# A decode kernel's key and value tiles, each loaded in two halves on two queues

## The chip, the cores and the metric

The kernel runs on one core of one Trainium2 chip. The metric is the device time of one execution in microseconds. The time before is the median of three runs, 663.4 us (663.39 to 663.56).

## The reference

The layer adds three things: its input, an attention over a long cache for one new token, and a small gated MLP. There are 4 sequences (B), 32 heads (H) of 128 elements (Dh), 4096 cached positions (S) and a model width D of 640. All tensors are bf16.

```
xn  = layernorm(x)                                  # x: 4 x 1 x 640
q   = (xn @ wq) as 4 x 32 x 1 x 128
s   = einsum("bhqd,bhkd->bhqk", q, k_cache) / sqrt(128)
o   = einsum("bhqk,bhkd->bhqd", softmax(s), v_cache)
A   = o as 4 x 1 x 4096 @ wo
z   = gelu(xn @ w_in);  z1, z2 = halves of z        # 640 -> 1728 -> 2 x 864
B   = (z1 * (w_sp * layernorm(z2) + b_sp)) @ w_out
out = x + A + B
```

k_cache and v_cache have 4 x 32 x 4096 x 128 elements each, 134 MB each. Every element is read once and used for one multiply and add, so almost all the bytes that the kernel moves are these two.

## The kernel before

**Tiles.** The 32 heads are cut in eight groups of four. One group of one sequence is a tile, so there are NT = 32 key tiles and 32 value tiles, numbered i = 4 * group + sequence. A tile is contiguous in memory, 4 MB, and is laid over 128 lanes, each of which holds NC = 128 positions ("chunks") of one head, that is 16384 elements or 32 KB. HC = NC / 2 = 64 chunks are half of a lane.

**Slots.** Keys and values share a pool of KV_SLOTS = 5 slots of 32 KB a lane (`kv`, function `slot`). At the start three of them hold the weights: two hold wq, one holds w_in and w_out.

**Loads.** The function `load` takes a slot and starts the transfer of one tile on SyncE's queue (line 123). It is one transfer of 128 lanes by 32 KB, except for the last value tile, which goes in four cuts at the chunks V_CUTS = (0, 64, 96, 112, 128), so that work on it can begin before all of it is there. The list `loads` gives the order: k0, k1, v0, k2, v1, k3, and so on, with a second key tile in a row at two places (EXTRA_K), so that the values end last. `pump` walks along this list and starts a load when the slot's former tile has been marked in `used`. Pieces of the output weight `wo` (640 KB each, line 159; the last one in four parts, line 157) go on SyncE's queue too, after the loads of every fourth iteration, and two more at the end. ScalarE's queue carries only x, two scalars and half of the output.

**The loop.** Under `manual_schedule` the instructions of TensorE (PE), VectorE (DVE), ScalarE (ACT) and SyncE (SP) stand in each engine's stream in the order in which the Python code calls them. One iteration i does, for key tile i and, one step behind, value tile j = i - 1 (from the two extra key tiles on, two and three steps behind):

- `product(i, 0)` and `product(i, 1)` (L457, DVE): each half of the keys times the query, in place.
- `fold_half(i, 0/1)` (L466, DVE): adds the upper 64 of 128 elements to the lower 64, in place.
- `sums(i, 0/1)` (L475, PE): adds what is left down to 8 columns, with the identity as weights; `row_sums` (L486, DVE) adds these.
- For tile i - 1: `lane_max` (L495, DVE), `lay_max` (L501, ACT), `spread_max` (L508, PE), `head_max` (L515, DVE), then `exps` (L524, ACT; and L533 on GpSimd (POOL), which lays the probabilities out in `pm`).
- `blocks(j)` (L548, PE): the probabilities times value tile j, into `pv_acc`. After each second tile ACT copies it out (L558) and `gather` (L569, PE) picks the parts.
- At the end of the iteration `used` gets value tile j and key tile i, and `pump` runs: it starts the loads of v(i+1), into the slot that value tile j leaves, and of k(i+3), into the slot of key tile i.

After the loop come the last softmax, `blocks(30)`, the first cut of `blocks(31)`, `pairs` for the other cuts (L581), and the projections with the last two `wo` pieces (L647).

**Waits of a transfer.** A transfer that is issued waits, on the issuing engine's stream, for the instructions that last read its slot. It also takes one of eight completion semaphores in turn, and waits until that semaphore's former transfer has landed. What stands behind it in that engine's stream waits with it.

**The start.** x is loaded on ACT's queue; wq, w_in and w_out on SP's. ACT computes `rstd` of the layernorm (L251) first; PE then waits for wq (`q_ps`, L285), `stage_q(0)` spreads the first queries, and `gmlp()` does the mixer, all ahead of `product(0, 0)` in DVE's stream.

Of the kernel before, what the change touches and what calls it, by code (L numbers as in the profile page):

```python
# [21 lines left out]
def kernel(  # L22
# [14 lines left out]
    nc = tc.nc  # L37
# [13 lines left out]
    NT = HG * Bsz  # L51
    LN = P // HT
    NC = HT * S // P
    HC = NC // 2
# [25 lines left out]
    def slot(name):  # L80
        return kv.tile([P, SLOT], BF16, tag="kv", name=name)
# [27 lines left out]
    def kv_view(cache, i):  # L109
        hg, b = divmod(i, Bsz)  # L110
        return cache[b, HT * hg : HT * (hg + 1)].rearrange("h s d -> (h s) d").rearrange(
            "(p c) d -> p (c d)", c=NC
        )

    k_tiles, v_tiles = {}, {}
    V_CUTS = (0, 64, 96, 112, NC)

    def load(which, i):
        cache, tiles = (A_k_cache, k_tiles) if which == "k" else (A_v_cache, v_tiles)
        t = slot("k_nat" if which == "k" else "v_nat")  # L120
        cuts = V_CUTS if (which, i) == ("v", NT - 1) else (0, NC)
        for c0, c1 in zip(cuts, cuts[1:]):
            nc.sync.dma_start(  # L123
                out=t[:, c0 * Dh : c1 * Dh], in_=kv_view(cache, i)[:, c0 * Dh : c1 * Dh]
            )
        tiles[i] = t[:].rearrange("p (c d) -> p c d", d=Dh)
# [13 lines left out]
    def pump():  # L140
        while n_loaded[0] < len(loads):
            at = n_loaded[0] + 3 - KV_SLOTS
            if at >= 0 and occupants[at] not in used:
                return
            load(*loads[n_loaded[0]])
            n_loaded[0] += 1
# [134 lines left out]
    for c in range(DC):  # L281
        t, i = wq_parts[c]
# [488 lines left out]
```

## Time and profile before

| what | value |
|---|---|
| median of 3 runs | 663.4 us |
| the profiled execution's own time | 663.4 us |
| its span on the core | 661.6 us |
| busy: PE / DVE / POOL / ACT | 53% / 74% / 23% / 7% |
| bytes moved, mean rate | 282.57 MB, 427 GB/s |
| mean granted TensorE clock | 0.726 |

The span runs from the first to the last instruction of the profiled execution, and the execution's own time is 1.8 us longer. Each engine's busy time is without its waits. In the profile, L123 is line 123 of the kernel before; SPq and ACTq are instructions of those engines' sequencers, which issue transfers; q1 is SP's queue and q10 ACT's. A view that lists waits gives the waiting group, who released it, the time in total, the number of times and the longest. A line of the timeline gives the start, the duration, the engine and line, the tiles written and read, and in brackets the engine's idle time before it and who ended it. A line of the transfers gives the number of issues, KB of each and the median time from issue to landing.

### The profile page before, as it was taken

How to read it: one execution, taken by the hardware profiler on the slowest of the kernel's cores; microseconds unless marked ns; L12 is line 12 of the kernel's file. 1: busy time of each engine (PE TensorE's matmuls, PEld its weight loads, DVE VectorE, ACT ScalarE, POOL GpSimd, SP SyncE). 2: the span in 40 equal slices, each digit the busy share in tenths (PEclk: the TensorE clock that was granted, in tenths of full speed). 3: DMA queues.
4: the chain of work that ended last, by engine and by line, in shares of the span. 5: the costliest groups of instructions: out<-in, count | busy, mean ns of one | idle time of the engine just before them, and what ended most of it. 6: DMA issues, size and time to landing. Idle time of an engine off the chain costs nothing.

```text
span 661.6 us, 5115 instructions
## 1 busy us (share of the span) xinstructions
PE 348.7 (53%) x2109; PEld 144.6 (22%) x2109; DVE 491.5 (74%) x334; ACT 49.3 (7%) x138; POOL 151.3 (23%) x57
## 2 busy tenths in 40 slices
PE   2526653646445455663745654465643756435567
PEld 1402211212121121221212222121211312112124
DVE  2299797867789677788776698776787899777950
ACT  0201100001000010001000000000100000000010
POOL 3002222112222112222112222112222133122230
PEclk9999676776767777766678657777576577688585
DMA  9999999999999999999999999999999999999997
GB/s 368 432 438 429 430 440 427 440 423 434 442 416 447 424 433 442 423 440 424 433 440 423 440 428 431 442 421 442 422 435 442 422 441 428 427 442 428 429 428 289
DMA packets 11971, 282.57 MB, mean 427 GB/s; under 512 B 1344, under 2 KB 1964, under 8 KB 3244
## 3 DMA queue, kind: packets, MB, share of 16 engines
q1 hardware_dynamic: 11928, 282.25, 99.2%
q8 instruction: 16, 0.26, 0.1%
q14 instruction: 7, 0.06, 0.0%
q10 hardware_dynamic: 20, 0.01, 0.0%
HBM read 282.24 MB, written 0.01 MB: 427 GB/s over the span
## 4 chain that ended last, share of the span: by engine, by line
issue 49%; DMA 25%; POOL 15%; DVE 7%; PE 3%; SPq 1%; ACT 0%; POOLq 0%; DVEq 0%; ACTq 0%
DMA k_nat<-in_A_k_cache_dram 20%; POOL pm L533 15%; DMA wo<-in_A_wo_dram 4%; DVE k_nat L457 4%; DVE k_nat L466 2%; PE s_ps L475 2%; PE pv_acc L548 1%; SPq L123 0%; DVE s_sb L486 0%; PE out_ps L647 0%; PE pv L569 0%; POOL own_sum L593 0%; DVE m L495 0%; SPq L92 0%; SPq L104 0%
## 5 line engine op out<-in xcount | busy, mean ns | idle before, releaser
L457 DVE TENSOR_TENSOR k_nat<-k_nat,qbc 128x8192 bf16<-128x8192 bf16 x64 | 282.8, 4419 | 97.8 <-DMA k_nat<-in_A_k_cache_dram 97.8
L533 POOL TENSOR_TENSOR pm<-p,hmask_bf 128x512 bf16<-128x512 bf16 x32 | 142.5, 4452 | 490.9 <-ACT p L524 490.9
L475 PE MATMUL s_ps<-k_nat,ident 128*128 128x512 bf16 x512 | 189.2, 536 | 68.2 <-DVE k_nat L466 68.2
L466 DVE TENSOR_TENSOR k_nat<-k_nat 128x4096 bf16<-128x4096 bf16 x64 | 151.8, 2372 | 0.0
L548 PE MATMUL pv_acc<-v_nat,pm 128*32 128x512 bf16 x1008 | 88.6, 514 | 39.1 <-POOL pm L533 35.5
L508 PE MATMUL max_ps<-lay,head_scale 128*128 128x32 f32 x64 | 18.7, 383 | 171.4 <-ACT lay L501 171.4
L475 PEld LDWEIGHTS <-ident 128*128 128x128 bf16 x512 | 67.9, 135 | 171.1 <-issue 153.8
L508 PEld LDWEIGHTS max_ps<-lay,head_scale 128*128 128x128 f32 x64 | 14.6, 284 | 186.0 <-ACT lay L501 186.0
L548 PEld LDWEIGHTS <-pm 128*32 128x32 bf16 x1008 | 30.2, 120 | 96.2 <-POOL pm L533 52.0
L486 DVE TENSOR_REDUCE s_sb<-s_ps 128x64 f32<-128x512 f32 x64 | 43.3, 677 | 4.2 <-PE s_ps L475 4.2
L501 ACT ACTIVATE lay<-lane_diag,m 128x32 f32<-128x32 f32 x32 | 10.3, 321 | 395.9 <-DVE m L495 395.9
L602 DVE RECIPROCAL rden<-den 128x16 f32<-128x16 f32 x8 | 2.1, 257 | 32.2 <-PE den L600 32.2
L569 PE MATMUL pv<-sel,pv_sb 128*128 128x8 f32 x128 | 19.4, 279 | 9.3 <-ACT pv_sb L558 9.3
L569 PEld LDWEIGHTS pv<-sel,pv_sb 128*128 128x128 f32 x128 | 17.9, 217 | 17.2 <-ACT pv_sb L558 17.2
L524 ACT ACTIVATE p<-s_sb,nb 128x128 bf16<-128x128 f32 x32 | 12.9, 402 | 63.5 <-DVE nb L515 63.5
L558 ACT COPY pv_sb<-pv_acc 128x512 f32<-128x512 f32 x16 | 9.4, 585 | 91.8 <-PE pv_acc L548 91.8
L495 DVE TENSOR_REDUCE m<-s_sb 128x1 f32<-128x128 f32 x32 | 9.1, 286 | 1.1
L285 PE MATMUL q_ps<-wq,xnT 128*32 128x512 bf16 x40 | 4.5, 631 | 8.3 <-DMA wq<-in_A_wq_dram 8.3
L647 PE MATMUL out_ps<-wo,o_r 128*4 128x320 bf16 x56 | 8.0, 433 | 0.3 <-DMA wo<-in_A_wo_dram 0.3
L292 DVE CAST q_sb<-q_ps 128x512 bf16<-128x512 f32 x1 | 0.7, 691 | 9.3 <-PE q_ps L285 9.3
L515 DVE TENSOR_REDUCE nb<-max_ps 128x1 f32<-128x32 f32 x32 | 5.9, 183 | 0.9 <-PE max_ps L508 0.9
L607 DVE TENSOR_TENSOR o_n<-pv,rden 128x16 bf16<-128x16 f32 x8 | 1.3, 168 | 6.7 <-PE pv L581 6.7
(94 smaller groups left out, 91.4 us busy)
## 6 DMA issues: line engine op xcount, KB each, us to landing
k_nat<-in_A_k_cache_dram SPq DMA_DIRECT2D x32, 4096.0 KB, 37.9
v_nat<-in_A_v_cache_dram SPq DMA_DIRECT2D x31, 4096.0 KB, 33.6
wo<-in_A_wo_dram SPq DMA_DIRECT2D x7, 640.0 KB, 38.1
wq<-in_A_wq_dram SPq DMA_DIRECT2D x1, 4096.0 KB, 12.8
w_sb<-in_B_w_in_dram SPq DMA_DIRECT2D x1, 2160.0 KB, 19.5
v_nat<-in_A_v_cache_dram SPq DMA_DIRECT2D x1, 2048.0 KB, 24.5
wq<-in_A_wq_dram SPq DMA_DIRECT2D x1, 1024.0 KB, 14.8
v_nat<-in_A_v_cache_dram SPq DMA_DIRECT2D x1, 1024.0 KB
```

Source lines behind the costliest of these rows:

```text
L457: nc.vector.tensor_tensor(out=t, in0=t, in1=qbcs[i // Bsz][:, i % Bsz, None, :].to_broadcast([P, HC, Dh]), op=ALU.mult,)
L466: nc.vector.tensor_tensor(out=t[:, :, 0:HD2], in0=t[:, :, 0:HD2], in1=t[:, :, HD2:Dh], op=ALU.add)
L475: nc.tensor.matmul(out=s[:], lhsT=ident[:], rhs=t[:, :, g * RW : (g + 1) * RW], start=(g == 0), stop=(g == n - 1),)
L486: nc.vector.tensor_reduce(out=scores[i][:, half * HC : (half + 1) * HC], in_=sums_ps.pop((i, half))[:], axis=AX.X, op=ALU.add,)
L495: nc.vector.tensor_reduce(out=m1[:], in_=scores[i][:], axis=AX.X, op=ALU.max)
L501: nc.scalar.activation(out=d[:], in_=lane_diag[:], func=ACT.Copy, scale=maxes[i][:, 0:1])
L508: nc.tensor.matmul(out=ps[:], lhsT=head_scale[:], rhs=maxes[i][:], start=True, stop=True)
L524: nc.scalar.activation(out=p[:], in_=scores.pop(i)[:], func=ACT.Exp, bias=nb[:], scale=scale_qk, accum_out=acc[hg % NACC][:, b : b + 1],)
L533: nc.gpsimd.tensor_tensor(out=p_m[b][:, :, e : e + GC * HT].rearrange("p g (c h) -> p g c h", h=HT), in0=p[:].rearrange("p (g c) -> p g c" ...
L548: nc.tensor.matmul(out=pv_acc[g * LN : (g + 1) * LN, :], lhsT=pm[:, c // GC, :], rhs=v_nat[:, c : c + GC, :].rearrange("p c d -> p (c d)") ...
L558: nc.scalar.copy(out=pv_sb[:], in_=pv_acc[:])
L569: nc.tensor.matmul(out=pvs[hg][:, :, b - 1 : b + 1], lhsT=pv_sb[:, k * Dh : (k + 1) * Dh], rhs=sel[:, k, :, :], start=(k == 0), stop=stop ...
```

## The change

Every tile but the last value tile is loaded in two transfers of 128 lanes by 16 KB: the first 64 chunks of each lane on SyncE's queue, the other 64 on ScalarE's. The last value tile keeps its four cuts, all on SyncE's queue, and so do the weights.

```
     def load(which, i):
         cache, tiles = (A_k_cache, k_tiles) if which == "k" else (A_v_cache, v_tiles)
         t = slot("k_nat" if which == "k" else "v_nat")
-        cuts = V_CUTS if (which, i) == ("v", NT - 1) else (0, NC)
+        last = (which, i) == ("v", NT - 1)
+        cuts = V_CUTS if last else (0, HC, NC)
         for c0, c1 in zip(cuts, cuts[1:]):
-            nc.sync.dma_start(
+            eng = nc.scalar if c0 == HC and not last else nc.sync
+            eng.dma_start(
                 out=t[:, c0 * Dh : c1 * Dh], in_=kv_view(cache, i)[:, c0 * Dh : c1 * Dh]
             )
         tiles[i] = t[:].rearrange("p (c d) -> p c d", d=Dh)
```

As built, the streams of PE, DVE and POOL hold the same instructions in the same order. SP's stream has 63 transfers of half the size where it had 63 whole ones. ACT's stream has 63 transfers more: tile k0's half right behind `rstd`, k1's behind the copy of the first spread queries (L453), and in the loop those of v(i+1) and k(i+3) at the end of iteration i, behind `exps(i - 1)` and the copy L558 and ahead of `lay_max(i)`. There are still eight completion semaphores, so a transfer now waits for the one eight before it in a sequence in which most tiles count twice.

More of the change, by code (lines that the diff above doesn't have):

```diff
@@ L120, in load @@
         t = slot("k_nat" if which == "k" else "v_nat")
-        cuts = V_CUTS if (which, i) == ("v", NT - 1) else (0, NC)
+        last = (which, i) == ("v", NT - 1)
+        cuts = V_CUTS if last else (0, HC, NC)
         for c0, c1 in zip(cuts, cuts[1:]):
-            nc.sync.dma_start(
+            eng = nc.scalar if c0 == HC and not last else nc.sync
+            eng.dma_start(
                 out=t[:, c0 * Dh : c1 * Dh], in_=kv_view(cache, i)[:, c0 * Dh : c1 * Dh]
```

## Prediction

> **What bounds the kernel now.** I read the page's slices and queues first, then the transfers' time to landing, then the waits, then the last 60 us line by line. The page:
>
> ```profile
> span 661.6 us, 5115 instructions
> ...
> DMA  9999999999999999999999999999999999999997
> ...
> DMA packets 11971, 282.57 MB, mean 427 GB/s; under 512 B 1344, under 2 KB 1964, under 8 KB 3244
> ...
> q1 hardware_dynamic: 11928, 282.25, 99.2%
> ...
> q10 hardware_dynamic: 20, 0.01, 0.0%
> ```
>
> Every slice has the DMA engines 90% busy or more, but for the last. Queue 1 (SP's) holds them for 99.2% of 16 engines' span; queue 10 (ACT's) moves x and four small things. The window from 100 to 600 us moves 433 GB/s at a DMA share of 1.00. So the sum of packet times is the time, plus some 2 us before the first packet and 4 us after the last load. Is there ever too little queued?
>
> ```profile
> k_nat<-in_A_k_cache_dram SPq DMA_DIRECT2D x32, 4096.0 KB, 37.9
> v_nat<-in_A_v_cache_dram SPq DMA_DIRECT2D x31, 4096.0 KB, 33.6
> wo<-in_A_wo_dram SPq DMA_DIRECT2D x7, 640.0 KB, 38.1
> ```
>
> A tile of 4.19 MB needs 9.7 us at 433 GB/s, yet lands 34 to 38 us after its issue: three to four tiles are always queued. The waits say the same from the other side:
>
> ```profile
> ACT lay L501 <- DVE m L495: 395.9, 32, 23.3
> ...
> DVE k_nat L457 <- DMA k_nat<-in_A_k_cache_dram: 97.8, 25, 5.6
> ```
>
> DVE, the busiest engine (74%), waits some 4 us for nearly every k tile, and ACT idles 12.4 us (395.9/32) per tile ahead of `lay`. The page's chain gives "issue" 49% and POOL's `pm` 15%; with the queue never empty I read that as a pipeline paced by landings. The end, from the timeline:
>
> ```profile
> 606.54 4.43 DVE L457 TENSOR_TENSOR k_nat<-k_nat,qbc 128x8192 bf16<-128x8192 bf16 x1 [2.45 <-DMA k_nat<-in_A_k_cache_dram]
> ...
> 635.60 1.91 PE L548 MATMUL pv_acc<-v_nat,pm 128*32 128x512 bf16 x32 [0.53 <-DMA v_nat<-in_A_v_cache_dram]
> ...
> 639.17 1.89 PE L475 MATMUL s_ps<-k_nat,ident 128*128 128x512 bf16 x8
> ...
> 645.28 3.60 PE L548 MATMUL pv_acc<-v_nat,pm 128*32 128x512 bf16 x32 [2.30 <-DMA v_nat<-in_A_v_cache_dram]
> ...
> 650.15 1.90 PE L548 MATMUL pv_acc<-v_nat,pm 128*32 128x512 bf16 x16 [0.72 <-DMA v_nat<-in_A_v_cache_dram]
> ```
>
> k tile 30 lands at 606.5, and from there DVE works through tiles 30 and 31 with no idle time until 636.9, PE through blocks, sums and the last softmax. PE then waits for v tiles 29, 30 and the first cut of 31 only 0.53 + 2.30 + 0.72 = 3.5 us in all. So compute follows the DMA closely at the end: **slack 3.5 us**.
>
> The profiled execution took 663.4 us, 1.8 more than its span; that is also the median of the three runs, so sums are made against 663.4. About 0.2% (1.3 us) is what a measurement of this kernel can tell from no change.
>
> **The change part by part.**
>
> *Packets.* 63 tiles go from one transfer to two. The trace's packet records show one packet per lane and transfer: 32 KB takes 1213 ns, and the only 16 KB ones on this queue (the first cut of v tile 31) take 611 ns. Per engine and tile that is 8 x 1213 against 16 x 611: +72 ns; a second completion packet adds 9 ns. Times 63: **+5.1 us** at most. The records overlap slightly: in the steady part they sum to 1.0035 of the time, and where only 16 KB packets run (645 to 647 us) to 1.006. So a packet occupies about 1209 and 607.4 ns: 16 x 607.4 - 8 x 1209 = +46 ns, and with the rest of the completion packet's 9 ns some 50 ns; over 63 tiles about +3. I take **+2.8 us**, since it comes from the rate really reached. Ends: -2.5 (below, if turns hide the fixed part) to +5.1.
>
> *The turns between the queues.* The nearest row: from 6.57 to 10.21 us ACT's queue had two tiny transfers waiting beside wq's 32 KB packets. Its four packets (2 and 4 B) went at 6.567, 7.782, 8.998 and 10.213 us, one between every two of SP's, 1215 ns apart. So turns alternate one packet each, and a turn and back costs 2 ns beyond SP's 1213, packet included. Other rows are dearer: a 16 KB instruction fetch on q8 takes 879 to 1013 ns and the packet behind it 1681 to 1766, some 0.8 us lost. I take 0, from the ACT row, which is the queue used here; the dear end is a rival.
>
> *Equal turns, unequal queues.* This is the part I expect to hurt. A tile is usable when both halves are in. SP still carries all that ACT doesn't: 8.6 MB of weights at the start and seven `wo` pieces. A `wo` piece is 8 packets of 5 KB per engine; in their turns ACT sends 8 packets of 16 KB, a whole half tile (2.1 MB, 4.85 us). Each `wo` therefore sets SP's halves one half tile behind ACT's; six come before k tile 30, so the lag grows until ACT's queue runs dry. There, ACT holds just the two newest halves (4.2 MB). At 37.9 us x 433 GB/s, 16.4 MB are outstanding at an issue; landed halves that wait for their partner take the lag L from it. SP holds 16.4 - L - 4.2, ACT 4.2, and their difference is L: L = 4.0 MB, **9.3 us**. While it lasts no byte is lost: one non-empty queue fills the engines, and 12 MB stay queued. But k tile 30 is complete only L after its place in the total order. Ends 0 and 9.3; behind the sixth `wo` (issued 480.3) no new one comes, so ACT may run dry and SP regain some: I take **7.3 us**.
>
> *At the end.* SP alone holds v tile 31 and the last `wo`s, so total bytes still end in the same place (+2.8). Compute starts its last run from k tile 30 later by 7.3 + 2.6 (the share of packet cost by then) = 9.9 us; the 3.5 us of slack absorb their part. **+6.4 us**, which hides the +2.8 of the DMA's own end.
>
> *ACT's stream.* 63 triggers at 0.33 us (SP's own rows) make 21 us on an engine that is 7% busy. As built, a v and a k half stand behind `exps` and ahead of the next `lay`. The v half waits for `blocks` on PE, the k half for the sums of the old k tile: `lay` needs the next DVE reduction, which lies behind those sums and 4.4 us of product. A half waits also for the transfer eight before it on its semaphore, four tiles back, three where a `wo` lies between; on ACT that tile is, in the loop, nearly always one that DVE's product needs first. 0 us; without that cover 0.66 us per tile.
>
> *The start.* ACT issues tile 0's half after `rstd` (3.92 us) and takes turns with wq: w_in, at 21.1 us now, comes up to 4.9 us later, and with it the mixer; the first product then starts near 36 instead of 34.5. 30 us of queued loads cover it: 0. SP's shorter waits gain nothing.
>
> Sum: 663.4 + 6.4 = **669.8 us**.
>
> **Rivals.**
> 1. *Faster: the alternating turns hide each packet's fixed part.* The 16 and 32 KB records differ by 602 ns for 16 KB, so about 9 ns of each is fixed; in the ACT row above a 9 ns packet cost 2. If a 16 KB packet among turns costs 602, a tile's 16 cost 9632 against 8 x 1209 = 9672: -40 ns, x 63 = -2.5 us. With no lag (SP catching up whenever ACT's queue is empty) that is **660.9**. It decides only if the lag at k tile 30 is under the 3.5 us of slack. Against: six `wo`s. 11%.
> 2. *Packets alone, the halves in step*: **666.2**, or 668.5 with records that don't overlap. For it: ACT's queue is empty often, if ACT issues late. 15%.
> 3. *No change*: one set of engines, full either way: **663.4**. For it: DMA share 1.00 now. Against: 611 is more than half of 1213. 5%. The Trainium skill (DMA: Bandwidth & Descriptors, Rules for kernel authors) says that spreading DMAs over SP and ACT doesn't help bandwidth, since all run on the same 16 engines, and saves only issue time; by it the sum is 663.4, SP's 0.33 us issues being hidden. The trace agrees that the engines are full, and by its packet lengths differs on zero.
> 4. *A turn between two large packets costs something*: 10 ns a turn is 63 x 16 x 10 ns = 10 us, **680** with the lag; the q8 rows' 0.4 us a turn would be over 1000. For it, those rows; against, the ACT row. 10%.
>
> Forecast 59%, 667 to 675.
>
> **Numbers.** Likeliest 669.8. The range takes in rivals 2 and 3 in the main, the forecast and the mild part of rival 4: 663 to 680. Faster by over 0.2% is rival 1 with a little of 3: 0.12; within: 0.05; slower: the rest, 0.83.
>
> **What would show it.** Queue 10 with about 130 MB; 16 KB packets near twice the length by record while both queues wait, and a steady rate 0.3 to 0.5% under 433. ACT's halves landing some 10 to 20 us after issue, SP's over 30, and the product of an iteration waiting for SP's half. k tile 30's first product near 616; PE's waits for v at the end gone; a last slice emptier of DMA. Wrong if the halves land together, if the steady rate moves by over 1%, or if the end keeps its 3.5 us of waits.

## The result, and the profile after

The changed kernel takes 666.8 us (median of 4 runs, 666.39 to 667.34) against 663.5 before: a ratio of 1.0049, with a 95% interval of 1.0037 to 1.0062. It is slower by 3.3 us, where the prediction gave 6.4. The profiled execution took 666.4 us with a span of 664.6. The page's lines that answer to those of before:

```profile
span 664.6 us, 5294 instructions
...
DMA  9999999999999999999999999999999999999996
...
DMA packets 21044, 282.59 MB, mean 425 GB/s; under 512 B 2352, under 2 KB 2972, under 8 KB 4252
...
q1 hardware_dynamic: 11928, 150.13, 53.0%
...
q10 hardware_dynamic: 9092, 132.13, 46.5%
```

The same bytes go in 21,044 packets instead of 11,971, shared between two queues that together hold the engines for 99.5% of the span. The DMA is as full as before, and the span ends 3.0 us later. The transfers of the same page, with the median time from issue to landing last:

```profile
k_nat<-in_A_k_cache_dram ACTq DMA_DIRECT2D x32, 2048.0 KB, 22.2
k_nat<-in_A_k_cache_dram SPq DMA_DIRECT2D x32, 2048.0 KB, 37.3
v_nat<-in_A_v_cache_dram SPq DMA_DIRECT2D x32, 2048.0 KB, 32.5
v_nat<-in_A_v_cache_dram ACTq DMA_DIRECT2D x31, 2048.0 KB, 18.5
wo<-in_A_wo_dram SPq DMA_DIRECT2D x7, 640.0 KB, 42.1
```

ACT's halves land some 14 to 15 us sooner after their issue than SP's. A tile needs both, so the product waits for SP's half: DVE waits 25 times for a key tile as before, 100.7 us in all (97.8 before), but the longest wait is now 10.2 us (5.6 before). The end, from the timeline:

```profile
615.84 4.43 DVE L459 TENSOR_TENSOR k_nat<-k_nat,qbc 128x8192 bf16<-128x8192 bf16 x1 [2.47 <-DMA k_nat<-in_A_k_cache_dram]
...
642.30 3.84 PE L550 MATMUL pv_acc<-v_nat,pm 128*32 128x512 bf16 x64
...
647.80 1.89 PE L477 MATMUL s_ps<-k_nat,ident 128*128 128x512 bf16 x8
...
651.54 1.91 PE L550 MATMUL pv_acc<-v_nat,pm 128*32 128x512 bf16 x32
...
654.10 1.05 PE L550 MATMUL pv_acc<-v_nat,pm 128*32 128x512 bf16 x16
...
659.58 1.23 PE L649 MATMUL out_ps<-wo,o_r 128*4 128x320 bf16 x8 [0.55 <-DMA wo<-in_A_wo_dram]
```

Line against line: k tile 30's first product is 9.3 us later (615.84 against 606.54), the last sums 8.6 (647.80 against 639.17), the first cut of v tile 31 only 3.95 (654.10 against 650.15), and the output projection 2.9 (659.58 against 656.64). Compute starts its last run 9.3 us late and ends it 2.9 late. It has made good 6.4 us, more than the 3.5 us of waits for v, and those waits are gone from all three lines. Two of the blocks are also shorter: those of tile 30 take 1.91 us where they took 3.60, the first cut 1.05 where it took 1.90.

What ends last is told by the chain of waits in order of time (start, duration, what the time went to). Before, from its end:

```profile
628.55 28.05 DMA wo<-in_A_wo_dram
656.60 0.04 issue
656.64 2.34 PE out_ps L647 x16
```

And after:

```profile
609.98 33.19 DMA v_nat<-in_A_v_cache_dram
643.17 0.02 issue
643.19 16.34 DMA wo<-in_A_wo_dram
659.54 0.04 issue
659.58 2.34 PE out_ps L649 x16
```

In both kernels the end waits for the last pieces of `wo` to land: the DMA's own end sets the time, not the computation behind the late keys. By the packet records the last packet of the loads ends at 657.93 us before and at 660.79 after, some 2.9 us later. The margin is small, though: after, PE stood ready for the projection only 0.55 us ahead of `wo` (the bracket of that line). That the lag cost nothing is a reading so far; the experiments test it.

### The profile page after: what moved, and what is told of

It reads as the page before. It is cut to its first block, busy times and chain, and to the rows that moved or that the text cites. A ratio compares the mean times of both kernels' runs of the same rounds, so it can differ in the third digit from the quotient of the medians.

```text
span 664.6 us, 5294 instructions
## 1 busy us (share of the span) xinstructions
PE 346.4 (52%) x2109; PEld 142.6 (21%) x2109; DVE 491.6 (74%) x334; ACT 49.4 (7%) x138; POOL 151.3 (23%) x57
## 2 busy tenths in 40 slices
DMA packets 21044, 282.59 MB, mean 425 GB/s; under 512 B 2352, under 2 KB 2972, under 8 KB 4252
## 4 chain that ended last, share of the span: by engine, by line
issue 49%; DMA 23%; POOL 15%; DVE 9%; PE 3%; ACT 0%; POOLq 0%; ACTq 0%
POOL pm L535 15%; DMA k_nat<-in_A_k_cache_dram 13%; DVE k_nat L459 5%; DMA v_nat<-in_A_v_cache_dram 5%; DVE k_nat L468 3%; DMA wo<-in_A_wo_dram 2%; DMA wq<-in_A_wq_dram 2%; PE s_ps L477 1%; PE pv_acc L550 1%; DVE s_sb L488 1%; PE out_ps L649 0%; DVE m L497 0%; POOL own_sum L595 0%; ACT p L526 0%; DVE res L740 0%
## 5 line engine op out<-in xcount | busy, mean ns | idle before, releaser
L459 DVE TENSOR_TENSOR k_nat<-k_nat,qbc 128x8192 bf16<-128x8192 bf16 x64 | 282.8, 4419 | 100.7 <-DMA k_nat<-in_A_k_cache_dram 100.7
L477 PE MATMUL s_ps<-k_nat,ident 128*128 128x512 bf16 x512 | 194.1, 548 | 68.2 <-DVE k_nat L468 68.2
L550 PE MATMUL pv_acc<-v_nat,pm 128*32 128x512 bf16 x1008 | 84.2, 494 | 37.5 <-POOL pm L535 34.1
L526 ACT ACTIVATION_READ_ACCUMULATOR p<-s_sb,nb 128x1 f32 x32 | 6.0, 187 | 0.0
## 6 DMA issues: line engine op xcount, KB each, us to landing
k_nat<-in_A_k_cache_dram ACTq DMA_DIRECT2D x32, 2048.0 KB, 22.2
v_nat<-in_A_v_cache_dram ACTq DMA_DIRECT2D x31, 2048.0 KB, 18.5
```

The lines of the kernel that those rows point to most:

```text
L459: nc.vector.tensor_tensor(out=t, in0=t, in1=qbcs[i // Bsz][:, i % Bsz, None, :].to_broadcast([P, HC, Dh]), op=ALU.mult,)
L477: nc.tensor.matmul(out=s[:], lhsT=ident[:], rhs=t[:, :, g * RW : (g + 1) * RW], start=(g == 0), stop=(g == n - 1),)
L526: nc.scalar.activation(out=p[:], in_=scores.pop(i)[:], func=ACT.Exp, bias=nb[:], scale=scale_qk, accum_out=acc[hg % NACC][:, b : b + 1],)
L550: nc.tensor.matmul(out=pv_acc[g * LN : (g + 1) * LN, :], lhsT=pm[:, c // GC, :], rhs=v_nat[:, c : c + GC, :].rearrange("p c d -> p (c d)") ...
```

## The experiments

Three theories were set against each other. **Packets**: the halves cost what their smaller packets take from the DMA's rate, whatever the queues. **Lag**: the 3.3 us come from late keys, with a slack larger than 3.5 us. **Turns**: the second queue costs by itself. "Before" took 663.56 to 663.62 us (medians) beside these kernels, and the differences are against that.

**The changed kernel again**, on the chip of the next ones.

> The changed kernel itself, to have it on the chip of the next three. All theories: 666.4 to 667.3 us against 663.4, queue 10 with 132 MB, the last load's packets near 661 us, k tile 30's first product near 616 us.

Measured 666.85 us (666.34 to 666.98), ratio 1.0045 (1.0033 to 1.0058), k tile 30's first product at 616.00.

**Both halves on SP's queue.** Packets without a second queue, without lag:

```
-            eng = nc.scalar if c0 == HC and not last else nc.sync
+            eng = nc.sync
```

> Both halves of each tile on SP's queue: the shorter packets stay, the second queue goes. Theory 'packets' (the whole +3.3 us is the fixed part of 8 more packets and one more completion per tile and engine): 666.0 to 666.8 us, steady rate 430 to 431 GB/s from 100 to 600 us. Rival 'lag' (the cost is the late second half at the end): 663.4 to 664.5 us less what packets cost, and k tile 30's first product near 609 us (606.5 plus the packets alone). Rival 'turns' (changing between two queues costs rate): 663.4 us and 433 GB/s. On both of the first two, k tile 30 comes near 609 us, since nothing lags.

Measured 666.32 us (666.16 to 666.57), ratio 1.0040 (1.0026 to 1.0054): +2.75 us. The window from 100 to 600 us moves 430 GB/s. k tile 30's first product starts at 604.90, earlier than expected: `product(i, 0)` reads only the first half, which one queue brings half a tile ahead. Its last load packet ends at 660.77 us, where the changed kernel's ends at 660.79. Packets alone bring nearly all of the loss, with no late key at the end.

**Quarters on SP's queue.** The kernel before, with four transfers of 8 KB a lane per tile:

```
-        cuts = V_CUTS if (which, i) == ("v", NT - 1) else (0, NC)
+        last = (which, i) == ("v", NT - 1)
+        cuts = V_CUTS if last else (0, HC // 2, HC, HC + HC // 2, NC)
...
```

> Four transfers of 128 lanes by 8 KB per tile, all on SP's queue: 24 more packets and three more completions per tile and engine than before. Theory 'packets', from the records of 8 KB (309 ns) and 32 KB (1213 ns) less the overlap of some 4 ns a packet: 32 x 305.3 - 8 x 1209 = 98 ns and three completions of about 5 ns, 113 ns x 63 tiles = 7 us, so 670 to 671 us and a middle rate near 428 GB/s. Rival 'lag' and rival 'turns': no second queue, so 663.4 to 664 us.

Measured 672.36 us (672.25 to 672.68), ratio 1.0130 (1.0116 to 1.0145): +8.8 us, some 2 more than expected. Its window over the steady part (duration; busy time and count of PE, PEld, DVE, ACT, POOL; granted clock, DMA share, GB/s):

```profile
100.00:600.00 500.00, 262.43 (x1455) 104.34 (x1456) 385.52 (x230) 33.27 (x102) 119.16 (x33) 0.69 1.01 427
```

The same window of the kernel before, of the one with both halves on SP's queue, and of the changed kernel:

```profile
100.00:600.00 500.00, 265.52 (x1480) 106.07 (x1484) 388.74 (x230) 33.27 (x102) 121.82 (x33) 0.70 1.00 433
```

```profile
100.00:600.00 500.00, 279.83 (x1480) 110.41 (x1484) 386.11 (x230) 33.27 (x102) 121.88 (x33) 0.67 1.01 430
```

```profile
100.00:600.00 500.00, 261.41 (x1486) 103.72 (x1486) 383.78 (x228) 32.48 (x99) 118.67 (x33) 0.70 1.01 431
```

The rate falls with the size of the packets: 433 GB/s with 32 KB, 430 and 431 with 16 KB, 427 with 8 KB. Per engine, halves add 9 packets to each of 63 tiles (8 with data, one completion) and quarters 27: 2.75 us / 567 is 4.9 ns a packet, 8.8 / 1701 is 5.2 ns. The end of the loads says the same without the rest of the kernel: the last load packet ends at 666.25 us with quarters, 8.3 us later than before, 4.9 ns a packet. The cost goes with the number of packets.

**Whole tiles on two queues.** The kernel before, with keys on SP's queue and values on ACT's, in packets of 32 KB:

```
-            nc.sync.dma_start(
+            eng = nc.scalar if which == "v" and i < NT - 1 else nc.sync
+            eng.dma_start(
```

> Whole tiles of 32 KB a lane, keys on SP's queue and values (but for the last) on ACT's: two queues in turns, the packets of before. Theory 'packets': 433 GB/s in the middle and, if values and keys stay in step well enough, 663.4 to 664 us; a lag of one queue would show at k tile 30 and could add up to 4 us at the end. Rival 'turns': 431 GB/s in the middle, and 666 us or more. Rival 'lag': above 665 us if keys fall behind, with the middle at 433.

Its times spread widely (663.63 to 681.43, median 665.45, ratio 1.0030 with 1.0015 to 1.0045), so its verdict rests on the rate of the profiled execution, which took 663.63 us with a span of 661.8:

```profile
100.00:600.00 500.00, 260.62 (x1496) 106.52 (x1495) 390.35 (x233) 33.03 (x101) 121.37 (x33) 0.70 1.00 433
```

The two queues take 53.6% and 45.6% of the engines, in turns, at the rate of one queue. The end of the loads (the last load packet of each profiled execution) puts the two causes side by side:

| packets a lane | one queue | two queues |
|---|---|---|
| 32 KB | 657.93 us (before) | 657.97 us |
| 16 KB | 660.77 us | 660.79 us (changed) |

The changed kernel's second profiled execution has 661.51, so these ends are good to some 0.7 us. **Turns** falls: the packets' size costs, not the second queue.

**How much slack is there?** The kernel before, with the loads of k tiles 30 and 31 one place later in the order, and in a second kernel two places:

```
+    for kk in (NT - 1, NT - 2):
+        at_k = loads.index(("k", kk))
+        loads.insert(at_k + 1, loads.pop(at_k))
```

> The kernel before, one queue and 32 KB packets, with key tiles 30 and 31 one place later in the order of loads (behind v tile 28): k tile 30 lands 9.7 us later, near 616.2, as in the changed kernel, and nothing else is changed. It prices a late k tile 30 alone. With the 3.5 us of slack that the prediction took: +6.2 us, 669.6. With the slack that the changed kernel's trace suggests (PE's waits for the last values plus a faster TensorE clock, some 6 us): +3 us or less, 664 to 666.5. If late keys cost nothing: 663.4.

> As the one before, but two places later: k tile 30 lands 19.4 us later, near 626. Once the slack is used up every further us costs one: the difference to one place later is 9.7 us by every theory; 3.5 us of slack gives +15.9 us (679.3), 6 us of slack +13 us (676.5).

One place: first product at 616.46, 9.92 us later; median 666.37 us (664.6 to 670.7, ratio 1.0040, 1.0021 to 1.0060), so +2.8. Two places: at 626.11, 19.57 later; 676.03 us (674.4 to 676.31, ratio 1.0181, 1.0168 to 1.0194), so +12.5. The second step costs 9.66 us for 9.65 of delay, one for one: from the first on, the computation is the end. The slack is 9.92 - 2.8 = 7.1 and 19.57 - 12.5 = 7.1 us, twice the 3.5 taken. (The delay is that of the profiled executions; with their times, 666.49 and 676.31 against 663.4, it is 6.8 and 6.7.) The chain of the first of the two holds no transfer from the last key tiles on; its end:

```profile
654.93 0.40 PE den L603 x2
655.32 1.01 PE pv_acc L551 x16
...
656.40 0.59 ACT pv_sb L561
...
657.04 1.06 PE pv L572 x8
658.10 1.70 PE pv L584 x64
659.80 2.27 PE out_ps L650 x16
```

**Taking the lag away.** Three kernels move `wo` so that SP's queue does not carry it alone. First every second one of the loop's six on ACT's queue, then all six:

```
-        nc.sync.dma_start(out=wo_tiles[j][:].rearrange("p r n -> p (r n)"), in_=wo_r[j])
+        eng = nc.scalar if j % 2 == 0 and j < HG - 2 else nc.sync
+        eng.dma_start(out=wo_tiles[j][:].rearrange("p r n -> p (r n)"), in_=wo_r[j])
```

> The changed kernel with the wo pieces of groups 0, 2 and 4 on ACT's queue instead of SP's, so that each queue is set behind in turn and the lag between a tile's halves stays within about one half tile (some 5 us) in place of 8 to 18. Same packets, same two queues. Theory 'packets' (the lag is absorbed by slack at the end): k tile 30's first product 3 to 6 us earlier than 615.8, near 610 to 612, and the time unchanged, 666 to 667 us. Rival 'lag': 664 to 665 us. Rival 'turns': 666 to 667 us, as 'packets'.

> The changed kernel with all six wo pieces of the loop on ACT's queue: now ACT's halves are set behind, by a half tile at each, and the first half of a tile comes first. The lag should change its sign on the way (SP behind by some 8 us after the start, ACT behind by 10 to 20 us from the third or fourth piece on). Theory 'packets': 666 to 667.5 us again, the lag at k tile 30 absorbed while it is under some 6 us beyond the packets, a little more if it is larger. Rival 'lag': 668 to 672 us if ACT's lag at k tile 30 is larger than SP's 10 us was.

Every second one: 666.37 us (666.19 to 666.46, ratio 1.0040), but the lag only flips back and forth. By the packet records SP's half of k tile 30 ends 7.9 us behind ACT's, and its first product starts at 614.72; that tells nothing on the lag. All six: the sign turns, ACT's halves run 12 to 22 us behind in the middle, and the first product starts at 608.57, since that product reads only SP's half, which is now the early one. The times spread from 666.26 to 672.56 (median 668.9, ratio 1.0082, 1.0058 to 1.0106): shifting the lag to the other queue does not help. The median lies above the 666 to 667.5 us of "packets" and where the rival "lag" was expected, though ACT's half of k tile 30 landed only 8.1 us behind by the completion packets (613.56 against 605.43). The trace is of the fastest of the six executions, so what the longer ones wait for is not shown.

The third one puts the first `wo` whole on ACT's queue and cuts the next five in two column halves of 2,560 B a lane, one on each queue:

```
...
+        whole = wo_tiles[j][:].rearrange("p r n -> p (r n)")
+        if j == 0:
+            nc.scalar.dma_start(out=whole, in_=wo_r[j])
+        elif j < HG - 2:
+            half = HT * D // 2
+            nc.sync.dma_start(out=whole[:, :half], in_=wo_r[j][:, :half])
+            nc.scalar.dma_start(out=whole[:, half:], in_=wo_r[j][:, half:])
...
```

> The changed kernel with the loads of wo shared between the two queues, the first one whole on ScalarE's queue, the next five cut into two column halves (2,560 bytes a lane), one half on each queue. Both queues then carry nearly the same bytes, so the queue of SyncE should no longer lie half a tile behind: lag at k tile 30 within 4 us of none, first product of k tile 30 between 604 and 610 us. Theory 'packets' (the loads' end moves by +2.8 us from the smaller packets, whatever the queues): 666.0 to 666.8 us, no different from both halves on one queue (666.3). Theory 'lag costs time in addition to the packets': the time falls by what the lag had cost, below 665.5. Theory 'a second queue costs by itself': above 667.

Measured 666.73 us (666.61 to 666.77), ratio 1.0047 (1.0033 to 1.0060). The lag is gone: by the packet records SP's halves end 0.3 to 2.1 us ahead of ACT's from v tile 4 to k tile 31. Its timeline:

```profile
609.74 4.43 DVE L467 TENSOR_TENSOR k_nat<-k_nat,qbc 128x8192 bf16<-128x8192 bf16 x1 [3.14 <-DMA k_nat<-in_A_k_cache_dram]
...
659.73 1.23 PE L657 MATMUL out_ps<-wo,o_r 128*4 128x320 bf16 x8 [0.28 <-DMA wo<-in_A_wo_dram]
```

k tile 30 starts 6.1 us earlier than in the changed kernel (609.74 against 615.84), the projection at the same time (659.73 against 659.58), and the time is the same. So the changed kernel's lag itself costs nothing.

**Late keys on top of the change**, by the same lines as above:

> The changed kernel with k tiles 30 and 31 issued one place later in the order, so that the keys of tile 30 are late by the lag and by a tile at once: first product of k tile 30 near 625.5 us, 19.0 later than in the kernel before. Theory 'slack 7.0, and the two ends are alternatives' (the chain of computation from the late keys ends last, the packets' cost lies beside it): 663.4 + 19.0 - 7.0 = 675.4 us. Theory 'the packets' 2.8 come on top of the chain': 678 or more. Theory 'the lag costs nothing, whatever comes after it': 666.8 us, the changed kernel's own time.

Measured 676.39 us (675.35 to 677.39), ratio 1.0193 (1.0179 to 1.0207). The first product starts at 627.24, 20.7 us later than in the kernel before and 1.7 later than expected. For this profiled execution (677.29 us) alternatives give 663.4 + 20.7 - 7.0 = 677.1 us; with 2.8 for packets on top it would be 679.9. The two costs are **alternatives**: the later of two ends counts. Absorbing the lag has its limit just here: with 11.4 us more delay, nearly all of it shows (10.9 us between the profiled executions, 677.29 against 666.42). What does not show, 0.5 us, is as much as PE waited for `wo` in the changed kernel.

## Why the prediction was right in direction, and where it missed

**What held.** The DMA engines bound the kernel and still do. *Packets*: +2.8 us was taken, +2.75 measured with both halves on one queue. *Turns*: taken at 0, and 433 GB/s on alternating queues bears it out. The Trainium skill (DMA: Bandwidth & Descriptors, Rules for kernel authors) was right that a second queue brings no bandwidth; the time of 663.4 us that followed from it is missed by the packets' price.

*Equal turns, unequal queues*: k tile 30's first product was forecast near 616 and came at 615.84, and spreading `wo` evenly took 6.1 us of that away, so the cause is the one named. That the number came out so well is partly luck. By the completion packets SP's half of k tile 30 landed 12.4 us behind ACT's (615.48 against 603.13), where 7.3 was taken and 9.3 was the upper end. But the lag is not all delay: in the kernel with split `wo` SP's half lands 6.1 us earlier (609.41) and ACT's 7.4 us later (610.53). So 6.1 of the 9.3 us are the lag's, where 7.3 was counted, and 3.2 come from the rest, where 2.6 was.

*ACT's stream*: priced at 0, rightly. Once `lay` stands behind a transfer that ACT issues, 9.4 us for want of a `wo`, and the time shows nothing of it. The kernel with split `wo` shows how deep that cover is:

```profile
ACT lay L511 <- DMA v_nat<-in_A_v_cache_dram: 181.4, 13, 17.8
```

Thirteen times ACT stands behind a transfer, 181 us in all, and the end does not move.

*The start*: priced at 0 as well, rightly, though its delay was undersized: the first product came at 39.98 instead of 34.46, where about 36 was said.

**The step that failed: the slack of 3.5 us in "At the end".** The runs put 7.1 in its place, and by the prediction's own sum 9.9 - 7.1 is +2.8, level with the DMA's own end instead of above it. The delay was right within 0.6 us (9.3), the absorption was half of what there is, and so the +2.8 that should have been hidden is what ends last. Rival 2's price, 666.2, came out, but not by its mechanism: the halves were not in step, the lag was there and was covered.

Why 7.1? The 3.5 counted only the time in which PE waits for v. Behind those waits PE also runs slower. Before, `gather` in the last run takes 1.88 us, where the chain of the kernel with late keys above has 1.06 (its line `pv L572`), and the denominators 0.61, where it has 0.40:

```profile
648.82 0.61 PE L600 MATMUL den<-own_sum,ones_sq 128*128 128x16 f32 x2
...
652.79 1.88 PE L569 MATMUL pv<-sel,pv_sb 128*128 128x8 f32 x8 [0.74 <-ACT pv_sb L558]
```

The kernel before, from 645 to 655 us (columns as above):

```profile
645.00:650.00 5.00, 4.14 (x34) 1.81 (x34) 0.26 (x1) 0.00 (x0) 0.09 (x1) 0.50 0.97 408
650.00:655.00 5.00, 4.11 (x43) 2.72 (x43) 0.00 (x0) 0.58 (x1) 0.00 (x0) 0.50 1.01 413
```

and after:

```profile
645.00:650.00 5.00, 3.94 (x40) 1.90 (x28) 1.49 (x2) 0.59 (x1) 0.00 (x0) 1.00 1.02 437
650.00:655.00 5.00, 3.48 (x52) 1.70 (x52) 1.15 (x4) 0.81 (x3) 1.21 (x2) 1.00 0.96 403
```

The granted clock (last but two) is 0.50 where PE had waited and 1.00 where it had not. The blocks of tile 30 gain 3.60 - 1.91 = 1.7 us, the first cut of tile 31 0.85, `gather` 0.8 and the denominators 0.2: some 3.6 us, which with the 3.55 us of waits makes about 7.1. So, by these traces, the slack was larger than the waits that it shows because the work behind the waits ran slower too. Each of the three kernels with late keys has the clock at 1.00 for the last softmax and `gather` at 1.06 us; the kernel before, the one with split `wo` and the one with both halves on one queue, which wait for v two or three times in their last 30 us, have 0.50 and 1.87 to 1.88 at `gather`. One wait need not do it: with every second `wo` on ACT's queue PE waits 0.56 us ahead of the last softmax and keeps 1.00; with all six there it waits 4.27 us, runs at 0.50 from 644 to 648 us and is back at 1.00 from 652 to 656, for `gather`. (The changed kernel lies between, with 1.44: its clock falls at 656.4 us, in the middle of `gather`.) That the waits cause the lower clock is read from these traces; no run held the clock and changed the waits alone. The Trainium skill (TensorE: Matmul & The Clock Gate, Part 1) says that half rate is the default and some 3.4 us of sustained work release it. The traces agree as far as they go: after, PE works without a gap from 638.79 to 646.1 us, and the clock is 0.50 in the window to 640 us, 0.66 from 640 to 644 and 1.00 from 644 to 656.

**What else was said would show it.** 16 KB packets near twice their length by record: wrong, they take 611 ns as alone, so a record does not include the other queue's turn. The steady rate 0.3 to 0.5% lower: 432.5 to 430.6 GB/s by the packet records, 0.44%. PE's waits for v at the end: gone. ACT's halves 10 to 20 us after issue: 18.5 and 22.2. A last slice emptier of DMA: hardly (6 tenths against 7), since the end is still the DMA's.

**What stays open.** The changed kernel and the one with both halves on SP's queue differ by 0.5 us, less than can be told apart. The times that spread, with late keys, with all `wo` on ACT's queue and with whole tiles on two queues, belong to kernels whose computation ends last or close to the DMA's end; whether PE's clock, a lag between the queues or something else does it there is open, since only one execution of each was traced. With keys one place late, three of seven times lie near 664.7 us and three near 666.4. If the keys came equally late in all of them, the slack is not one fixed number: 7.1 by the median, nearer 9 in the faster ones. Two places late and late keys on top of the change agree with 7.

## What to carry to other kernels

Where a full DMA bounds a kernel, cut its transfers no finer than the work needs: packets cost about 5 ns each here, and a second queue gives nothing back. Slack wasn't the sum of the waits in the trace here: ask how fast the waiting engine would run without them, or better, follow the chain of waits and see which end is last; two causes that move the same end do not add, the later one counts. A tile split over two queues is only as early as its slower queue, so where that tile has no slack, what else a queue carries should be shared as evenly as the tile.

## What the runs showed of the hardware that was not expected

- The fixed cost per packet is about the same from 32 to 8 KB: 4.9 ns by the halves' time, 5.2 ns by the quarters' (5.0 and 4.9 by the end of the loads). These times carry some 0.9 us of uncertainty either way, so the halves' figure alone could be 3 to 6 ns.
- A record of a packet shows no waiting for the other queue: 611 ns for 16 KB, alone or in turns.
- TensorE's granted clock at the last `gather` was 0.50 in the three kernels that wait for v two or three times in their last 30 us, and 0.96 to 1.00 in the three with late keys, which do not; between the two lie some 3.6 us of 663, as much as all the waits there.
